# Fused attention and MLP on one Trainium2 core: global outputs kept in the score banks, AV of batches 0 and 1 unit by unit, the last output tile in two column halves

## The chip, the core and the metric

The kernel runs on one core of a Trainium2 chip. The metric is the time of one execution on the device, in microseconds (us); lower is better. Six runs of the kernel before gave 316.4 to 318.26 us, median 316.57 us.

The engines are named as in the profile: PE (TensorE matmul), PEld (its weight loads), DVE (VectorE), ACT (ScalarE), POOL (GpSimd) and SP (SyncE). A queue with a q at the end (SPq, ACTq, POOLq) is the part of an engine that issues its DMAs.

## The reference, cut to what matters

There are 8 batches, 8 heads, 512 local and 32 global tokens of 64 elements. Local queries see the 32 global keys and the local keys within 32 positions; global queries see everything. The result goes through a two-layer MLP.

```
s_g   = scale * q_g @ concat(k_g, k_l)^T            # 32 global queries x 544 keys
out_g = softmax(s_g) @ concat(v_g, v_l)
s_ll  = scale * q_l @ k_l^T, masked to |i - j| <= 32
s_lg  = scale * q_l @ k_g^T
out_l = softmax(concat(s_lg, s_ll)) @ concat(v_g, v_l)
x     = concat(out_g, out_l)                        # [8 * 544, 512]
h     = x @ w_in                                    # [4352, 2048]
out   = (h * sigmoid(1.702 * h)) @ w_out            # [4352, 512], float32
```

## The kernel before, in words

The program is written in the order in which each engine executes it: nothing reorders it, so an engine that waits holds back everything behind it in its own queue. Waits between engines come from the tiles that instructions read and write.

**Attention.** A `Quad` is four heads of one batch; quad `a` of a batch holds heads 0 to 3 and quad `c` heads 4 to 7. Its steps are methods:

- `T` (`Tk`, `Tq`) transposes keys and queries on DVE, and `ext` copies the global queries beside the local ones (four small DVE copies, one for each key window).
- `S(0)` and `S(1)` are the two rounds of score matmuls (16 each, row group by row group) into one 4-bank PSUM tile from the pool `psS`, which has a single buffer; `S(0)` ends with 8 small matmuls `gk` (global queries by global keys).
- `X` takes exp of a round on ACT (one large instruction, and in round 0 a small one for the `gk` columns), `M` multiplies the mask on DVE, `eg` builds a block-diagonal copy of the global part.
- `K` (8 matmuls) gives the scores of local queries by global keys in a bank `kb`, and `XK` its exp `ek`.
- `ekU(unit)` and `U(unit)` accumulate AV in a bank `ov` for each of three units: unit 0 is the row sum (ones as weights), units 1 and 2 the even and odd half of the values. `ekUs` does the three `ekU` in a row.
- `Gm` (16 + 4 matmuls) gives the global outputs in a bank `og`.
- `R` on DVE turns the row sum around, inverts it and spreads it (`sT`, `rT`, `rs`); `XL(0)` and `XL(1)` scale units 1 and 2 into the MLP input `xL`; `G` scales the global outputs into `xG` (three DVE instructions `rg`, `xg`, `xG`). `UG` is `ekUs`, the three `U` and `Gm`; `RXG` is `R`, `XL(0)`, `XL(1)`, `G`.

The banks `kb`, `ov`, `og`, and those of the MLP (`hp`, `op`), share a PSUM pool `psP` of 4 banks, handed out in turn.

**MLP.** `h_step(i, fc)` computes one of 16 blocks of the hidden layer of batch i: 4 matmuls of 128x512 into `hp`, tanh on ACT (`th`, two buffers), and one DVE instruction to `gT`. `o_mm` accumulates four of the 16 matmuls of one of the four output tiles of a batch in `op`; after the last of them `o_out` copies `op` to `ob` on ACT and SP issues four DMAs. Batch index 8 stands for the 256 global tokens of all batches.

**Order.** Batch 0's attention runs first, while the weights come in over POOL's DMA queue; PE runs dummy matmuls (`keep`) until the first scores are ready. Batch 1's attention is woven into the output tiles of batch 0 (`osteps`). From batch 2 on, `phase_o(i)` weaves the attention of batch i + 1 into the output tiles of batch i: `o(0)`, `c.S(0)`, `a.UG(c)`, `o(1)`, `c.S(1)`, `o(2)`, `a2.S(0)`, `c.UG(a2)`, `o(3)`, where `a2` is the first quad of batch i + 2; the hidden layer of batch i + 1 follows without interruption. In its last call there is no `a2`. The hidden layer of batch 1 contains `a.S(0)`, `a.K`, `a.X(0)`, `a.XK` of batch 2 after block 3, `M(0)` after 5 and `eg` after 7; `a.T` and `a.ext` of batch 2 stand ahead of block 0. At the end the hidden blocks of the global tokens alternate with the output tiles of batch 7, and the two output tiles of the global tokens come last.

Of the kernel before, what the change touches and what calls it, by code (L numbers as in the profile page):

```python
# [20 lines left out]
def kernel(  # L21
# [138 lines left out]
    def keep(n, ps):  # L160
        for _ in range(n):
            nc.tensor.matmul(ps, lhsT=warm[:, 0:128], rhs=warm, start=True, stop=True)

    keep(17, psP.tile([128, 512], F32, name="w", tag="p"))
# [43 lines left out]
    def transpose_g(lo, hi):  # L208
        for dst, s in ((kgT, rkg), (qgT, rqg)):
            nc.vector.transpose(dst[:, lo:hi, :32], s[:, lo:hi].bitcast(F32))  # L210
# [24 lines left out]
    class Quad:  # L235
        def __init__(self, Q):
# [11 lines left out]
            self.st = {}  # L248

# [16 lines left out]
        def ext(self):  # L266
            for (r0, nr), t0, n in zip(WIN, (0, 20, 1, 20), (4, 3, 3, 4)):
# [4 lines left out]
        def S(self, rnd, split=False, warm=0):  # L272
# [3 lines left out]
            else:  # L276
                pt = psS.tile([128, 4, 512], F32, name="s4")
# [15 lines left out]
            if rnd == 0:  # L293
                self.gk(ps[2][:, RW : RW + 32], self.qg)
# [14 lines left out]
        def X(self, rnd):  # L309
            e = self.E[rnd]  # L310
            if isinstance(self.ps, list):
                for j in range(4):
                    nc.scalar.activation(e[:, j, :RW], self.ps[j][:, :RW], AF.Exp, scale=scale)  # L313
                return
            nc.scalar.activation(e[:, :, :RW], self.ps[:, :, :RW], AF.Exp, scale=scale)  # L315
            if rnd == 0:
# [13 lines left out]
        def eg(self):  # L330
# [3 lines left out]
                self.E[0][:, 2, RW:].rearrange("p (o w) -> p o w", o=1).to_broadcast([128, 4, 32]))  # L334
# [15 lines left out]
        def ekUs(self, nxt=None):  # L350
            if nxt:
                nxt.K(0)
# [21 lines left out]
        def Gm(self):  # L374
            og = pbank("og")
# [36 lines left out]
        def UG(self, nxt=None):  # L412
            self.ekUs(nxt)
            for unit in range(3):
                self.U(unit)
            self.Gm()
# [46 lines left out]
    def o_out(i, tci, op):  # L463
        ob = moe.tile([128, d_model], F32, name="ob", bufs=6)
        nc.scalar.activation(ob, op, AF.Copy, scale=0.5)  # L465
        if i < B:
            rows = out[i * S + Sg : (i + 1) * S, :].rearrange("(r t) m -> t r m", t=16)
            for j in range(4):
                nc.sync.dma_start(out=rows[4 * tci + j], in_=ob[32 * j : 32 * j + 32, :])
        else:  # L470
            for j in range(4):
                r = (4 * tci + j) * S
                nc.sync.dma_start(out=out[r : r + Sg, :], in_=ob[32 * j : 32 * j + 32, :])
# [18 lines left out]
    cast_g32(0, "qk")  # L492
    transpose_g(0, 2)
    a.ext()
    a.Tq(0, 8)
    a.Tq(8, 16)
    a.Tk((0, 1))
    a.Tk((2, 3))
    load_rest()
# [10 lines left out]
    c.Tq()  # L510
    c.S(0)
# [4 lines left out]
    a.ekUs(c)  # L516
# [12 lines left out]
    c.eg()  # L529
    gTs[0] = moe.tile([128, FC, TB], BF16, name="gT")  # L530
    pt = pts[0] = psS.tile([128, 4, 512], F32, name="s4")
    c.ekUs()
    for unit in range(3):
        c.U(unit)
    c.R()
    for fc in range(4):
# [40 lines left out]
    a.S(0)  # L577
    a.K()
# [4 lines left out]
    osteps(0, (0, 2), (0, 3))  # L583
# [143 lines left out]
```

The softmax here doesn't subtract the row's maximum and nothing guards it: scores larger than these inputs give would overflow.

## Time and profile before

| | |
|---|---|
| median of six runs | 316.57 us (316.4 to 318.26) |
| the profiled execution's own time | 316.4 us |
| its span, first to last instruction | 314.7 us |
| PE busy / DVE busy / ACT busy / POOL busy | 298.3 / 211.0 / 165.8 / 79.9 us |
| instructions on PE / DVE / ACT | 3154 / 462 / 253 |
| mean granted PE clock | 0.995 of full speed |

Outside the span lie 1.7 us of the profiled execution's own time. A matmul's end in the profile is modelled: 128x512 matmuls are shown 379 ns long, but follow each other every 0.216 us, so a PE that is shown busy can still have lost time between two starts. A row of the timeline gives start, time until the last end, engine, line, operation, output <- inputs, shape, how many were merged (x), and in brackets the idle time before it and who ended it. A few per cent of the matmul records are missing, so a count of 15 can stand for 16.

### The profile page before, as it was taken

How to read it: one execution, taken by the hardware profiler on the slowest of the kernel's cores; microseconds unless marked ns; L12 is line 12 of the kernel's file. 1: busy time of each engine (PE TensorE's matmuls, PEld its weight loads, DVE VectorE, ACT ScalarE, POOL GpSimd, SP SyncE). 2: the span in 40 equal slices, each digit the busy share in tenths (PEclk: the TensorE clock that was granted, in tenths of full speed). 3: DMA queues.
4: the chain of work that ended last, by engine and by line, in shares of the span. 5: the costliest groups of instructions: out<-in, count | busy, mean ns of one | idle time of the engine just before them, and what ended most of it. 6: DMA issues, size and time to landing. Idle time of an engine off the chain costs nothing.

```text
span 314.7 us, 7687 instructions
## 1 busy us (share of the span) xinstructions
PE 298.3 (95%) x3154; PEld 144.4 (46%) x3189; DVE 211.0 (67%) x462; ACT 165.8 (53%) x253; POOL 79.9 (25%) x131
## 2 busy tenths in 40 slices
PE   6779999999999999999999999999999998999993
PEld 2344444444554455444454455445454454446651
DVE  7787946977866866776857866776677755673310
ACT  4717483386536745466446645566356650663420
POOL 8912588676146000900054002100000000000000
PEclk9999999999999999999999999999999999999998
DMA  8999999999969211970289113901120022101122
GB/s 154 156 196 205 207 158 180 166 133 108 164 77 164 47 35 44 155 106 18 53 79 172 20 35 69 102 0 35 36 60 10 0 52 52 33 2 33 35 67 68
DMA packets 59907, 27.44 MB, mean 87 GB/s; under 512 B 43232, under 2 KB 51424, under 8 KB 59872
## 3 DMA queue, kind: packets, MB, share of 16 engines
q0 software_dynamic: 51536, 17.11, 50.2%
q1 hardware_dynamic: 7904, 9.25, 12.0%
q10 hardware_dynamic: 432, 0.59, 0.6%
q8 instruction: 25, 0.41, 0.6%
q14 instruction: 10, 0.08, 0.1%
HBM read 35.13 MB, written 8.91 MB: 140 GB/s over the span
## 4 chain that ended last, share of the span: by engine, by line
PE 73%; DMA 10%; POOL 8%; DVE 4%; issue 2%; ACT 1%; POOLq 0%; ACTq 0%
PE op L458 34%; PE hp L433 30%; DMA w_out_sb<-in_moe_w_out_dram 9%; PE s L286 4%; POOL rk L84 3%; DVE sT L391 3%; POOL v L97 2%; PE ov L347 2%; PE ov L368 2%; DMA v<-in_v_l_dram 2%; POOL w_in_sb L217 1%; DVE gT L441 1%; ACT th L440 1%; PE kb L305 0%; PE s L305 0%
## 5 line engine op out<-in xcount | busy, mean ns | idle before, releaser
L458 PE MATMUL op<-w_out_sb,gT 128*128 128x512 bf16 x519 | 123.2, 379 | 2.9 <-DVE xL L400 0.8
L441 DVE SCALAR_TENSOR_TENSOR gT<-th,hp 128x512 bf16<-128x512 f32 (+1 forms) x140 | 91.0, 656 | 42.4 <-ACT th L440 41.7
L433 PE MATMUL hp<-xL,w_in_sb 128*128 128x512 bf16 x487 | 108.2, 379 | 0.6
L440 ACT ACTIVATE th<-hp 128x512 f32<-128x512 f32 (+1 forms) x140 | 79.9, 573 | 43.1 <-PE hp L433 39.3
L433 PEld LDWEIGHTS <-w_in_sb 128*128 128x128 bf16 x576 | 56.1, 98 | 65.1 <-issue 1.3
L458 PEld LDWEIGHTS <-gT 128*128 128x128 bf16 x544 | 51.6, 98 | 59.1 <-issue 4.1
L465 ACT ACTIVATE ob<-op 128x512 f32<-128x512 f32 x34 | 20.3, 597 | 77.6 <-PE op L458 77.5
L315 ACT ACTIVATE e<-s 128x1712 bf16<-128x1712 f32 x31 | 49.4, 1595 | 6.0 <-PE s L305 5.5
L97 POOL DMA_DIRECT2D v<-in_v_l_dram x36 | 26.9, 753 | 95.0 <-PE og L385 88.8
L84 POOL DMA_DIRECT2D rk<-in_k_l_dram x64 | 34.9, 557 | 15.5 <-DMA w_in_sb<-in_moe_w_in_dram 5.9
L391 DVE STREAM_TRANSPOSE sT<-ov 128x512 f32<-128x512 f32 x16 | 11.5, 717 | 34.4 <-PE ov L368 34.4
L322 DVE TENSOR_TENSOR e<-e,mask 128x1408 bf16<-128x1408 bf16 x32 | 27.9, 872 | 7.1 <-ACT e L315 6.9
L286 PE MATMUL s<-q,kT 32*128 32x200 bf16 (+1 forms) x512 | 21.3, 284 | 2.7 <-DVE kT L256 1.4
L400 DVE TENSOR_TENSOR xL<-ov,rs 128x512 bf16<-128x512 f32 x32 | 20.7, 684 | 1.5
L286 PEld LDWEIGHTS <-kT 32*128 32x128 bf16 x512 | 11.0, 95 | 16.8 <-issue 10.1
L338 ACT ACTIVATE ek<-kb 128x512 bf16<-128x512 f32 x16 | 9.6, 603 | 7.0 <-PE kb L305 7.0
L368 PE MATMUL ov<-e,v 128*32 128x192 bf16 (+1 forms) x512 | 12.5, 239 | 0.0
L347 PE MATMUL ov<-ek,rvg 32*32 32x512 bf16 x128 | 10.0, 375 | 1.9 <-DVE xL L400 1.9
L395 DVE STREAM_TRANSPOSE rs<-rT 128x512 f32<-128x512 f32 x16 | 11.4, 711 | 0.6
L256 DVE STREAM_TRANSPOSE kT<-rk 128x512 f32<-128x512 f32 (+1 forms) x17 | 11.3, 669 | 0.1
L259 DVE STREAM_TRANSPOSE q<-rq 128x512 f32<-128x512 f32 (+1 forms) x17 | 10.9, 644 | 0.3 <-DMA rq<-in_q_l_dram 0.3
L305 PE MATMUL kb<-q,kgT 32*32 32x512 bf16 x128 | 10.0, 385 | 0.6 <-ACT e L313 0.6
(64 smaller groups left out, 142.5 us busy)
## 6 DMA issues: line engine op xcount, KB each, us to landing
out_dram<-ob SPq DMA_DIRECT2D x136, 64.0 KB, 1.8
rk<-in_k_l_dram POOLq DMA_DIRECT2D x64, 64.0 KB, 4.2
v<-in_v_l_dram POOLq DMA_DIRECT2D x28, 128.0 KB, 4.4
rq<-in_q_l_dram POOLq DMA_DIRECT2D x6, 512.0 KB, 6.8
w_in_sb<-in_moe_w_in_dram POOLq DMA_DIRECT2D x4, 512.0 KB, 11.8
w_out_sb<-in_moe_w_out_dram POOLq DMA_DIRECT2D x4, 512.0 KB, 13.4
rq<-in_q_l_dram POOLq DMA_DIRECT2D x3, 256.0 KB, 8.0
q<-in_q_l_dram ACTq DMA_DIRECT2D x1, 512.0 KB, 4.1
```

The source lines that it names most:

```text
L84: nc.gpsimd.dma_start(out=loaded[b][0][32 * j : 32 * j + 32, u], in_=kf[b, j][:, u])
L97: nc.gpsimd.dma_start(out=vtiles[b % 2][p, s, :, :, :D], in_=vf[b, t][:, hs])
L286: nc.tensor.matmul(ps[j][:, off : off + n * nr], lhsT=self.k[p, 128 * c : 128 * c + 128, e], rhs=self.q[p, t0 : t0 + n, r0 : r0 + nr, e], ...
L315: nc.scalar.activation(e[:, :, :RW], self.ps[:, :, :RW], AF.Exp, scale=scale)
L322: nc.vector.tensor_mul(e, e, mask[:, rnd : rnd + 1, :].to_broadcast([128, 4, LW]))
L391: nc.vector.transpose(sT.rearrange("p a b -> p (a b)"), self.st[0])
L400: nc.vector.tensor_mul(self.x[:, 2 * self.u + h, :], self.st[1 + h], self.st["rs"])
L433: nc.tensor.matmul(hp[:, : width(i)], lhsT=w_in_c[:, fc // 8, kc, fc % 8 // 2, :, fc % 2], rhs=(xL[i] if i < B else xG)[:, kc, :], start=( ...
L440: nc.scalar.activation(th[:, :n], hp[:, :n], AF.Tanh, scale=0.851)
L441: nc.vector.scalar_tensor_tensor(gTs[i][:, fc, :n], in0=th[:, :n], scalar=1.0, in1=hp[:, :n], op0=ALU.add, op1=ALU.mult)
L458: nc.tensor.matmul(op, lhsT=gTs[i][:, fc, tci * 128 : tci * 128 + 128], rhs=w_out_sb[:, fc, :], start=(first and fc == 4 * f4), stop=(fc = ...
L465: nc.scalar.activation(ob, op, AF.Copy, scale=0.5)
```

## The change

- The dummies ahead of the first scores: 62 of 128 columns in the place of 17 of 512.
- The start of batch 0: cast and transpose of the global keys move behind the transposes of queries and local keys, and two of the four `ext` copies behind the first half of the key transpose. In the split round `S(1)` of quad 0 `gk` now comes with that round, and its exp takes the extra columns of bank 2; the small separate exp goes.
- `gk` is a step of its own (`gg`) at the head of `ekUs(nxt)`, or after `a.S(0)`; it writes to the same place of the score tile as before.
- `Gm(nxt)` writes the global outputs to 66 free columns of bank 0 of the next quad's score tile, in the place of a bank of `psP`; `RXG` of a quad now stands behind `XK` and `X(0)` of the next one in the program.
- AV of the second quad of batch 0 and of batch 1, and of the last quad, goes unit by unit (`ekU(0)`, `U(0)`, `ekU(1)`, `U(1)`, ...).
- Batch 1's steps and batch 0's output tiles are woven in another order. In the hidden layer of batch 1, `a.T` of batch 2 moves from ahead of block 0 to behind block 3, the transposes of the globals and `ext` behind block 5, `S(0)`, `gg`, `K`, `XK`, `X(0)` behind block 7, `M(0)` and `eg` behind block 10.
- The last output tile is computed in two halves of 256 columns, each with its own bank, copy and four DMAs; in the second half two of the DMAs are issued by ACT.

```diff
-    keep(17, psP.tile([128, 512], F32, name="w", tag="p"))
+    keep(62, psP.tile([128, 512], F32, name="w", tag="p"), 128)
...
+        def spt(self, rnd):
+            if rnd or self.pt is None:
+                pt = psS.tile([128, 4, 512], F32, name="s4")
+                if rnd:
+                    return pt
+                self.pt = pt
+            return self.pt
+
+        def gg(self):
+            self.gr = 0
+            self.gk(self.spt(0)[:, 2, RW : RW + 32], self.qg)
...
         def ekUs(self, nxt=None):
             if nxt:
+                nxt.gg()
                 nxt.K(0)
...
-        def Gm(self):
-            og = pbank("og")
+        def Gm(self, nxt=None):
+            og = nxt.pt[:, 0, RW : RW + D + 2] if nxt else pbank("og")
...
         def UG(self, nxt=None):
-            self.ekUs(nxt)
+            if nxt:
+                self.ekUs(nxt)
             for unit in range(3):
+                if not nxt:
+                    self.ekU(unit)
                 self.U(unit)
-            self.Gm()
+            self.Gm(nxt)
...
+        last = i == B and tci == B // 4 - 1
+        for lo, hi in ((0, 256), (256, 512)) if last else ((0, 512),):
+            if last:
+                op = pbank("op")
+                for fc in range(FC):
+                    nc.tensor.matmul(op[:, lo:hi], lhsT=gTs[i][:, fc, tci * 128 : tci * 128 + 128],
+                                     rhs=w_out_sb[:, fc, lo:hi], start=(fc == 0), stop=(fc == FC - 1))
+            nc.scalar.activation(ob[:, lo:hi], op[:, lo:hi], AF.Copy, scale=0.5)
             for j in range(4):
+                eng = nc.scalar if lo and j % 2 else nc.sync
...
-    cast_g32(0, "qk")
-    transpose_g(0, 2)
-    a.ext()
+    cast_g32(0, "q")
+    transpose_g(0, 2, "q")
+    a.ext((0, 1))
     a.Tq(0, 8)
     a.Tq(8, 16)
     a.Tk((0, 1))
+    a.ext((2, 3))
     a.Tk((2, 3))
+    cast_g32(0, "k")
+    transpose_g(0, 2, "k")
...
-    c.ekUs()
     for unit in range(3):
+        c.ekU(unit)
         c.U(unit)
     c.R()
+    c.eg()
...
     a.S(0)
+    a.gg()
     a.K()
...
-    osteps(0, (0, 2), (0, 3))
+    osteps(0, (2, 1), (2, 0), (0, 2), (0, 3))
     a.S(1)
     a.X(1)
     c.T()
     a.M(1)
     osteps(0, (1, 2), (1, 3))
+    osteps(0, (2, 2))
     c.S(0)
-    c.X(0)
-    c.M(0)
-    c.eg()
-    osteps(0, (2, 0), (2, 1), (2, 2), (2, 3))
-    c.S(1)
-    c.X(1)
+    osteps(0, (2, 3))
     a.ekUs(c)
     c.XK()
-    for unit in range(3):
-        a.U(unit)
+    c.X(0)
+    a.U(0)
+    a.R()
+    osteps(0, (3, 0))
+    a.U(1)
+    a.U(2)
+    c.S(1)
     a.Gm()
-    a.R()
-    c.M(1)
     a.XL(0)
     a.XL(1)
     a.G()
-    osteps(0, (3, 0), (3, 1))
+    c.M(0)
+    c.eg()
+    c.X(1)
+    c.M(1)
+    osteps(0, (3, 1), (3, 2))
     c.UG()
     c.RXG()
-    osteps(0, (3, 2), (3, 3))
+    osteps(0, (3, 3))
     a, c = nq[2]
-    a.T()
-    transpose_g(4, 6)
-    a.ext()
...
     for fc in range(FC):
         h_step(1, fc)
         if fc == 3:
+            a.T()
+        if fc == 5:
+            transpose_g(4, 6)
+            a.ext()
+        if fc == 7:
             a.S(0)
+            a.gg()
             a.K()
+            a.XK()
             a.X(0)
-            a.XK()
-        if fc == 5:
+        if fc == 10:
             a.M(0)
-        if fc == 7:
             a.eg()
...
         c.S(0)
         a.UG(c)
-        a.RXG()
         c.XK()
         c.X(0)
+        a.RXG()
...
             c.UG(a2)
+            a2.XK()
+            a2.X(0)
         else:
...
-            c.ekUs()
             for unit in range(3):
+                c.ekU(unit)
                 c.U(unit)
...
-    for st in range(FC // 2):
+    for st in range(4):
         o_mm(B, st)
+    o_out(B, 1, None)
```

## The prediction

> **What bounds the kernel now.** The page first: PE is busy in every slice from the third on, at the full clock, so a change counts only where PE starts a matmul later than it could.
>
> ```profile
> PE   6779999999999999999999999999999998999993
> PEclk9999999999999999999999999999999999999998
> ```
>
> The waits of PE name the stalls: banks of `psP` that DVE has not read yet (L347, L458), and the first scores (L286).
>
> ```profile
> PE ov L347 <- DVE xL L400: 1.9, 3, 1.0
> PE s L286 <- DVE kT L256: 1.4, 1, 1.4
> PE op L458 <- DVE xL L400: 0.8, 1, 0.8
> ```
>
> Then the timeline, at the places that the change touches. The start: first scores, second half of w_in, and the matmuls that need it.
>
> ```profile
> 8.28 0.67 PE L286 MATMUL s<-q,kT 32*128 32x200 bf16 x16 [1.43 <-DVE kT L256]
> 21.89 0.10 PEld L433 LDWEIGHTS <-w_in_sb 128*128 128x128 bf16 x1 [0.18 <-DMA w_in_sb<-in_moe_w_in_dram]
> 22.40 1.89 PE L433 MATMUL s<-xL,w_in_sb 128*128 128x512 bf16 x8 [0.20 <-DVE xL L400]
> ```
>
> The hidden layer of batch 1 (ACT's tanh, DVE's gT, then the scores of batch 2):
>
> ```profile
> 58.19 3.62 PE L433 MATMUL hp<-xL,w_in_sb 128*128 128x512 bf16 x16
> 59.25 0.60 ACT L440 ACTIVATE th<-hp 128x512 f32<-128x512 f32 x1 [0.27 <-PE hp L433]
> 61.13 2.69 DVE L441 SCALAR_TENSOR_TENSOR gT<-th,hp 128x512 bf16<-128x512 f32 x4
> 61.74 0.66 PE L286 MATMUL s<-q,kT 32*128 32x200 bf16 x16
> ```
>
> A later batch, from unit 0 of `a` to `c.S(1)`:
>
> ```profile
> 113.87 0.49 PE L368 MATMUL ov<-e,ones 128*32 128x160 bf16 x16
> 114.41 0.72 DVE L391 STREAM_TRANSPOSE sT<-ov 128x512 f32<-128x512 f32 x1 [2.31 <-PE ov L368]
> 114.93 0.20 PE L385 MATMUL og<-rvg,eg 128*32 128x66 bf16 x4
> 115.18 3.61 PE L458 MATMUL op<-w_out_sb,gT 128*128 128x512 bf16 x15
> 117.66 0.28 DVE L407 TENSOR_SCALAR xg<-og,rg 128x64 bf16<-128x64 f32 x1
> 118.72 0.67 PE L286 MATMUL s<-q,kT 32*128 32x228 bf16 x16
> ```
>
> The last quad, and the end:
>
> ```profile
> 264.43 0.38 PE L458 MATMUL op<-w_out_sb,gT 128*128 128x512 bf16 x1 [0.80 <-DVE xL L400]
> 306.77 5.28 SPq L473 DMA_DIRECT2D out_dram<-ob  x8
> 309.60 0.60 ACT L465 ACTIVATE ob<-op 128x512 f32<-128x512 f32 x1 [2.86 <-PE op L458]
> ```
>
> **Later batches: 11 x 0.12 = 1.32 us gained.** Four `og` matmuls are followed by the next work after 0.125 us when nothing is waited for (24.36 to 24.50), but by `op` after 0.25 (114.93 to 115.18): `op` gets the bank of unit 0 and waits for `sT`, which ends at 115.13. With `og` out of `psP`, the built order gives `op` the bank of `kb`, freed by XK (113.81 + 0.60 = 114.41): no wait. This happens twice in each of five `phase_o` and once in the sixth. What is late next: in the score bank `Gm` stands before X(0) in the program, and X(0) (one access over all four banks) waits for it, so X(0) moves from 114.30 to 115.2, its small exp ends at 117.0; `rg` waits for that, but starts at 117.47 anyway; `c.S(1)` now waits for `xg`, done at 117.95, and wants to start at 118.72 - 0.12 = 118.60. Slack 0.65, cost nothing. The Trainium skill ("PSUM — Partial Sum Buffer", PSUM bank collisions raise a hardware error) speaks against this placement: two engines may not touch one bank in the same partitions at once, whatever the columns, so `Gm` and X(0) must take turns. In the rows `og` at 114.80 to 115.13 lies inside X(0) (114.30 to 115.89), in different banks; by the rule the turn costs ACT 0.9 us, which is the move already counted, and PE nothing.
>
> **Start: 0.43 us gained, not more.** Ahead of the first scores DVE loses one cast, one transpose and two copies. From the cast of the queries (done 6.24): transpose 6.28, two copies 6.53 and 6.63, two query transposes 6.73 and 7.09, first half of the keys 7.42 to 7.82; first scores 7.87 for 8.28. The landed keys (four DMAs, the last at 7.03) allow it. `gk` no longer stands before X(0): 8.60 for 9.15; quad 1's scores 11.80 for 12.35, its X(0) 12.52 for 13.22, its `S(1)` 14.25 for 14.96, its `ekU(0)` 15.74 for 16.45. There unit by unit acts: `U(0)` waits for the mask of round 1 (`M(1)` on DVE, done 17.75), unit 1 follows at 17.97, unit 2 needs the bank of `XL(1)` (18.36), and PE is through at 19.3 for 20.5. The 8 hidden matmuls on the first half of w_in end at 21.03; the second half of w_in lands at 21.85 whatever PE does (the row at 21.89 waits for it). They go on at 21.97 for 22.40, since `xL` is then ready at 20.8. So 0.86 us of the lead is lost to the DMA, and it also covers the dummies. These run 0.427 us each until 4.62 us, when the clock is granted, then 0.216. No row has 128 columns with full weights; bounds are a quarter of 512 columns (0.107 and 0.055) and the length of a weight load (0.147 and 0.098): the train would end at 6.4 or at 8.7. I take 6.4, since weight loads lie beside matmuls in all rows; at 8.7 the first scores come 0.8 later, still under the cover. The skill's "TensorE: Matmul & The Clock Gate" (Back-to-back issue gap) has two figures for 128 columns, 56 ns isolated and 81 ns sustained; by them the train would end at 6.4 or 7.3, both before 7.87; no run here shows it.
>
> **Batch 1: 0.43 shrinks to 0.14.** Scores at 38.26 for 38.68. Four groups of four `op` matmuls (0.863 each, 0.10 for a change of shape) put `S(1)` at 43.02; `w_out` for the third and fourth group has landed (37.7, 40.2) long before. Three more groups, `c.S(0)` at 46.31, `op(2, 3)` to 47.87. Three `op` tiles now hold banks: `ekU(2)` waits for the copy of the third (its last matmul ends 47.94, copy to 48.58), costing 0.27; `U(0)` at 48.94, `sT` at 49.48. From `sT` to the end of `xG` DVE takes 3.75 (the spacings 55.41 to 59.16), and only then come `c.M(0)` (53.23 to 54.10) and, after `eg`, `c.M(1)` (54.13 to 55.02). PE has `op(3, 0)`, units 1 and 2, `c.S(1)`, `Gm` and two groups, done at 53.6, then `ekU(0)`; `c.U(0)` waits for both masks until 55.08, about 1.0 lost. Its `sT` starts at 55.46. Unit by unit costs two more changes of shape, some 0.2; `op(3, 3)` ends at 57.6, but the hidden layer's first bank is that of unit 1, read by `XL(0)` until 58.00. It starts at 58.05 for 58.19. The old stalls of this stretch (about 2 us, at `og`, `ekU`, `op`) are thus replaced.
>
> **Hidden layer of batch 1: from 0.14 ahead to 0.87 behind.** This is where the change costs. A `gT` starts 1.70 after its step does (59.89 for the step at 58.19: 0.86 + 0.20 + 0.60 + 0.04). Steps take 0.863, so gT3 starts at 62.35, `a.T` behind it runs 62.95 to 64.18, gT4 and gT5 follow at 0.60 each, the transposes at 65.38, the first `ext` copy ends at 65.87. `a.S(0)` stands on PE behind block 7, which is through at 65.05: it waits 0.87. Before, the copies were done at 61.2 when PE arrived at 61.64. After it X(0) (1.59) and XK (0.60) stand before tanh 8, and the two `th` buffers tie tanh n to gT n - 2; with `M(0)` (0.77) behind gT10 the bank of block 15 comes free 0.3 late and that of block 12 0.1 late. The stall of 0.27 that this layer had goes. Together 1.0 lost; `S(1)` at 74.56 for 73.69.
>
> **Last quad: 0.45.** Before, three `ekU` take 0.757 before `U(0)`; now one takes 0.305. The chain sT, rT, rs, `XL(0)` (2.55) that frees the bank of the next `op` starts 0.45 earlier, and PE arrives before it ends, so all of it shows.
>
> **End: 0.8.** Matmuls of 256 columns follow each other every 0.109, so two halves cost what the whole did; the last ends 0.04 later. The copy takes 0.38 for 0.60 (tanh of 256 columns as the row). Four issues at 0.36 to 0.47 put the last one 1.30 after the first, landing 1.81 later at 313.33; now SP still has the first half's DMAs to issue until about 310.3, then two; the last starts near 310.75 and lands at about 312.5.
>
> **Sum.** 0.87 - 1.32 - 0.45 - 0.80 = -1.70, from 316.40 to 314.70 in the profiled execution; its time is 0.17 under the median of 316.57, so 314.9 as a median. A measurement here tells 0.3%, 0.95 us, from no change: faster is below 315.62, slower above 317.52.
>
> **Rivals.** (1) `a.S(0)` in the hidden layer does not wait: DVE gets to the copies in time. For it: gT's mean is 656 ns and some start early; against it: the 1.70 of every step. Worth 0.87: 314.0. Chance 0.18. (2) DVE's backlog there grows: from gT4 on 12 steps at the unhidden 0.69 in place of 0.60 add up to 1.1, and every tanh behind X(0) hands it on; 316.0, no change. Chance 0.20. (3) Slower: `c.S(1)` waits for `xg` in the shared score bank in six batches. It decides from 0.65 us of delay in the chain sT to xg; at 1.1 it costs 0.45 x 6 = 2.7 and the time is 317.6. Against it: DVE is idle before `sT` (2.31 in the row). Chance 0.05. The forecast keeps 0.57. That the change does not do what it says is excluded by the built order, which shows `op` waiting for XK.
>
> Range: down to rival 1 with 0.7 more if the start and batch 1 stall less than worked out, 313.3; up through rival 2 to 316.3.
>
> **What would show it.** Right: no 0.12 gap after `og`; the start held by w_in at 21.9; a wait of PE s on DVE q near 65 of about 0.9; SP's last issue near 310.7 less the gain. Wrong: a wait of `s` for `xg` in every batch, a clock granted later than 4.6, or `S(1)` of batch 2 earlier than 73.7.

## The result, and the profile after

The changed kernel takes 315.06 us (median of 24 runs, 313.95 to 316.32), where the kernel before, run beside it, takes 317.44 us (median of 50 runs, 316.21 to 320.97). The ratio is 0.9929, with a 95% interval of 0.9915 to 0.9943: 0.6 to 0.9% faster. The profiled execution of the changed kernel takes 314.89 us, 1.51 us less than that of the kernel before (316.40); their spans are 313.2 and 314.7 us. The forecast was 314.9 us, in a range of 313.3 to 316.3.

The page shows what it showed before: PE busy almost everywhere and the clock granted.

```profile
PE   8679999889999999999999999999999999999994
PEclk9999999999999999999999999999999999999999
```

The waits of PE (total us, times, longest us) are what has changed. The banks of `psP` that DVE had not read (1.9, 0.8 and parts of others before) are gone. In their place stand two transfers, the masks, and the `ext` copies.

```profile
PE ov L387 <- DVE e L328: 1.1, 2, 0.6
PE s L455 <- DMA w_in_sb<-in_moe_w_in_dram: 0.8, 1, 0.8
PE ov L387 <- DMA v<-in_v_l_dram: 0.8, 1, 0.8
PE s L291 <- DVE q L273: 0.7, 1, 0.7
```

The timeline of the changed kernel at the places that the prediction showed; first the start. The first scores come 0.37 earlier. But U(1) of quad 0 now waits for v, and the hidden matmuls on the second half of w_in wait for that half and start at 22.40, as before.

```profile
7.90 0.67 PE L291 MATMUL s<-q,kT 32*128 32x200 bf16 x16
15.85 0.80 PE L387 MATMUL ov<-e,v 128*32 128x160 bf16 x32 [0.80 <-DMA v<-in_v_l_dram]
19.92 1.67 PE L455 MATMUL s<-xL,w_in_sb 128*128 128x512 bf16 x7 [0.16 <-issue]
22.40 1.90 PE L455 MATMUL s<-xL,w_in_sb 128*128 128x512 bf16 x8 [0.81 <-DMA w_in_sb<-in_moe_w_in_dram]
```

The hidden layer of batch 1: eight blocks in one row, then the scores of batch 2, which wait for the copies of `ext`, a second wait (0.19) for the bank of the last block, and `S(1)` at 74.86 for 73.69.

```profile
58.42 7.07 PE L455 MATMUL hp<-xL,w_in_sb 128*128 128x512 bf16 x32
66.19 0.67 PE L291 MATMUL s<-q,kT 32*128 32x200 bf16 x16 [0.71 <-DVE q L273]
73.91 1.02 PE L455 MATMUL hp<-xL,w_in_sb 128*128 128x512 bf16 x4 [0.19 <-DVE gT L463]
74.86 0.67 PE L291 MATMUL s<-q,kT 32*128 32x228 bf16 x16
```

A later batch: `op` starts 0.13 behind the start of the four last matmuls of the global outputs (now `s<-rvg,eg`, since they lie in the score bank), in place of 0.25. `X(0)` waits for them (0.80), as worked out, and `xg`, done at 118.90, is 0.7 ahead of `c.S(1)`.

```profile
115.89 0.20 PE L404 MATMUL s<-rvg,eg 128*32 128x66 bf16 x4
116.02 3.63 PE L480 MATMUL op<-w_out_sb,gT 128*128 128x512 bf16 x15
116.17 1.60 ACT L321 ACTIVATE e<-s 128x1712 bf16<-128x1712 f32 x1 [0.80 <-PE s L404]
118.62 0.28 DVE L426 TENSOR_SCALAR xg<-s,rg 128x64 bf16<-128x64 f32 x1
119.58 0.67 PE L291 MATMUL s<-q,kT 32*128 32x228 bf16 x16
```

The last quad (no wait in front of `op`), and the end: a copy of 0.38, and ACT issues two of the DMAs of the second half.

```profile
264.02 3.63 PE L480 MATMUL op<-w_out_sb,gT 128*128 128x512 bf16 x16
302.92 7.97 SPq L502 DMA_DIRECT2D out_dram<-ob  x14
309.25 0.38 ACT L494 ACTIVATE ob<-op 128x256 f32<-128x256 f32 x1 [1.36 <-PE op L492]
309.66 0.82 ACTq L502 DMA_DIRECT2D out_dram<-ob  x2
```

Stage by stage, from the starts of PE's rows (the last landing from the transfers):

| mark | before | after | lead so far | lead forecast |
|---|---|---|---|---|
| first scores | 8.28 | 7.90 | 0.37 | 0.41 |
| hidden matmuls, second half of w_in | 22.40 | 22.40 | 0.00 | 0.43 |
| first scores of batch 1 | 38.68 | 38.60 | 0.08 | 0.42 |
| first hidden matmul of batch 1 | 58.19 | 58.42 | -0.23 | 0.14 |
| `S(1)` of batch 2 | 73.69 | 74.86 | -1.17 | -0.87 |
| `c.S(1)` of batch 7 | 257.24 | 257.25 | -0.01 | 0.45 |
| first hidden matmul of batch 7 | 267.88 | 267.49 | 0.39 | 0.90 |
| last landing | 313.33 | 312.05 | 1.28 | 1.70 |

### The profile page after: what moved, and what is told of

Same layout as the page of the kernel before. It is cut to its first block, busy times and chain, and to the rows that moved or that the text cites. A ratio compares the mean times of both kernels' runs of the same rounds, so it can differ in the third digit from the quotient of the medians.

```text
span 313.2 us, 7832 instructions
## 1 busy us (share of the span) xinstructions
PE 299.5 (96%) x3214; PEld 148.9 (48%) x3250; DVE 210.8 (67%) x462; ACT 167.2 (53%) x253; POOL 79.9 (26%) x131
## 4 chain that ended last, share of the span: by engine, by line
PE 84%; DVE 5%; DMA 4%; POOL 3%; issue 2%; ACT 2%; DVEq 0%; POOLq 0%; ACTq 0%
PE op L480 35%; PE hp L455 33%; PE s L291 5%; PE ov L387 5%; DMA w_in_sb<-in_moe_w_in_dram 4%; PE ov L365 2%; POOL rk L84 1%; DVE gT L463 1%; PE op L492 1%; POOL v L97 1%; ACT th L462 1%; PE kb L310 1%; DVE e L328 1%; PE s L455 1%; PE s L310 1%
## 5 line engine op out<-in xcount | busy, mean ns | idle before, releaser
L480 PE MATMUL op<-w_out_sb,gT 128*128 128x512 bf16 x503 | 119.8, 380 | 1.8 <-issue 0.8
L480 PEld LDWEIGHTS <-gT 128*128 128x128 bf16 x528 | 49.1, 98 | 56.2 <-issue 3.5
L494 ACT ACTIVATE ob<-op 128x512 f32<-128x512 f32 (+1 forms) x35 | 20.5, 585 | 64.5 <-PE op L480 62.0
L387 PEld LDWEIGHTS <-v 128*32 128x32 bf16 x512 | 9.9, 97 | 2.9 <-issue 2.9
```

The costliest lines, as they stand in the source:

```text
L387: nc.tensor.matmul(ov[32 * j : 32 * j + 32, :].rearrange("p (t r) -> p t r", t=16)[:, :, r0 : r0 + nr], lhsT=lv, rhs=self.E[c // 2][:, j, ...
L480: nc.tensor.matmul(op, lhsT=gTs[i][:, fc, tci * 128 : tci * 128 + 128], rhs=w_out_sb[:, fc, :], start=(first and fc == 4 * f4), stop=(fc = ...
L494: nc.scalar.activation(ob[:, lo:hi], op[:, lo:hi], AF.Copy, scale=0.5)
```

## The experiments

Unless said otherwise each kernel is the changed one with the edit that is shown. In their traces the stretches from batch 1 on that an edit does not touch repeat within 0.02 us from kernel to kernel, so a stretch between two marks can be compared directly. There is one exception: in the first of the two last versions batch 1 takes 19.97 for 19.81, because PE waits 0.16 for the last quarter of w_out, which lands at 41.87. The ratios are to the kernel before, in runs on the same chip.

### The weave in the hidden layer of batch 1, alone undone

```diff
+    a.T(); transpose_g(4, 6); a.ext()      # ahead of block 0
     for fc in range(FC):
         h_step(1, fc)
...
-        if fc == 7:
+        if fc == 3:
             a.S(0); a.gg(); a.K()
...
```

> The changed kernel with one part undone: in the hidden layer of batch 1 the steps of batch 2 stand again where they stood before (transposes and ext ahead of block 0, scores, K and exps behind block 3, mask behind 5, eg behind 7). My theory: this weave is the part that costs. In the changed kernel the stretch from the first hidden matmul of batch 1 to S(1) of batch 2 takes 16.45 us, before it took 15.51; undone, it should take 15.5 again, the wait of PE s on DVE q (0.7 in the waits of PE, behind the last ext copy) should be gone, and the time be 0.94 us below the changed kernel's: about 0.989 to 0.990 of the kernel before, where the changed one has 0.993. Rival: the weave was moved because batch 1's second quad now ends later on DVE (its R, XL, G); then the transposes and ext, put back ahead of block 0, hold up gT 0 to 3, PE waits for banks there, and the stretch stays at 16.2 to 16.5, time unchanged.

Measured: ratio 0.9922 (0.9902 to 0.9943), median 314.37 us, profiled execution 314.03 us. The start happens to be the same (block 4 at 24.52 and 24.51), and so is the first hidden matmul of batch 1 (58.42 in both). From there to `S(1)` of batch 2 pass 15.57 us for 16.45:

```profile
58.42 3.61 PE L455 MATMUL hp<-xL,w_in_sb 128*128 128x512 bf16 x16
61.97 0.66 PE L291 MATMUL s<-q,kT 32*128 32x200 bf16 x16
63.17 10.88 PE L455 MATMUL hp<-xL,w_in_sb 128*128 128x512 bf16 x48
73.99 0.67 PE L291 MATMUL s<-q,kT 32*128 32x228 bf16 x16
```

The row at 61.97 has no idle time ahead of it: the wait for `ext` is gone. The weave costs 0.88 us in the trace, and the rival, that DVE's later end of batch 1 takes it back, falls. The ratio's interval alone would not have told it from the changed kernel.

### Global outputs in the pool again

```diff
-            self.Gm(nxt)
+            self.Gm()
```

> The changed kernel with one part undone: the global outputs of all quads go to a bank of the pool psP again; every other order stays. My theory: from batch 2 on, 'op' behind the 'og' matmuls gets the bank of unit 0 again and waits for sT, 0.12 us each time (0.25 in place of 0.125 from the last og to op), 11 times: 1.2 to 1.3 us slower than the changed kernel, about 0.997 of the kernel before. Rival: the score bank gives something else too or instead (X(0) of the next quad is held by Gm and reorders ACT); then the spacing behind og does not change and the time moves by less than 0.5.

Measured: ratio 0.9980 (0.9956 to 1.0005), median 316.16 us. `op` waits again and starts 0.25 behind the start of the four last `og` matmuls, at eleven places from batch 2 on:

```profile
116.19 0.20 PE L404 MATMUL og<-rvg,eg 128*32 128x66 bf16 x4
116.44 3.61 PE L480 MATMUL op<-w_out_sb,gT 128*128 128x512 bf16 x16
```

From `S(1)` of batch 2 to `c.S(1)` of batch 7 the kernel before takes 183.55 us, this one 183.54, the changed one 182.39. So the whole lead of the later batches, 1.15 us or 11 times 0.105, belongs to this one edit.

### The last output tile in one piece

```diff
-        for lo, hi in ((0, 256), (256, 512)) if last else ((0, 512),):
...
+        nc.scalar.activation(ob, op, AF.Copy, scale=0.5)
...
-    for st in range(4):
-        o_mm(B, st)
-    o_out(B, 1, None)
+    for st in range(FC // 2):
+        o_mm(B, st)
```

> The changed kernel with one part undone: the last output tile is computed, copied and stored in one piece again. My theory: the last matmul ends 0.04 earlier, the copy takes 0.60 in place of 0.38, and four issues on SP of 0.36 to 0.47 follow it, so the last landing comes 3.75 to 3.85 us after the last matmul's start, where the halves have it at about 2.95: 0.85 to 0.9 us slower than the changed kernel, 0.9955 to 0.996 of the kernel before. Rival: the end is set by the transfers alone (1.6 to 1.8 us from issue to landing) and the halves only gain the copy's 0.22: 0.2 to 0.3 slower.

Measured: ratio 0.9972 (0.9954 to 0.9989). From the first hidden matmul of the globals to the last landing pass 31.64 us, in the changed kernel 30.75: the halves are worth 0.90. The copy alone saves 0.22. Another 0.48 is the chain of issues: the last one starts 1.33 behind the end of the last copy here, where all four are on SP, and 0.85 behind it in the changed kernel. The last transfer saves 0.24: it carries half as much in the changed kernel and lands 1.57 behind its issue, for 1.81 here. The last copy starts 0.04 later there, which takes a little back.

```profile
303.16 8.73 SPq L494 DMA_DIRECT2D out_dram<-ob  x12
309.44 0.60 ACT L487 ACTIVATE ob<-op 128x512 f32<-128x512 f32 x1 [2.86 <-PE op L480]
```

### The halves alone, in the kernel before

The same edit the other way round, in the kernel before.

> The kernel before with one part of the change alone: the last output tile in two column halves. My theory: 0.85 to 0.9 us faster than the kernel before (0.997), all of it behind the last hidden matmul of the globals; the stretch from the first hidden matmul of the globals to the last landing falls from 31.64 to 30.75. It also shows the start of the kernel before a second time: if v lands at 11.8, 12.8, 13.8, 14.8 and the second half of w_in at 21.85 again, the later landings of the changed kernel (12.2, 14.0, 15.2, 15.7; 22.36) come from the change; if it shows the late ones too, they change from execution to execution, and the first hidden matmuls of batch 0 still follow the same path, since they wait for xL at 22.4 there. I expect the second. Rival for the end: less than 0.3 gained, since the transfers set the end.

Measured: ratio 0.9991 (0.9962 to 1.0021), which decides nothing; the trace does: 30.74 us for 31.64 from the first hidden matmul of the globals to the last landing, 0.90 again. The start of the kernel before is seen a second time here: v lands at 12.75, 13.75, 14.73 and 15.63 (11.81 to 14.75 in its first profile), the second half of w_in at 22.09 (21.85), and the hidden matmuls on it start at 22.54, still held by `xL`. So late landings come in the kernel before too, and cost it little.

### The start as before

```diff
-    keep(62, psP.tile([128, 512], F32, name="w", tag="p"), 128)
+    keep(17, psP.tile([128, 512], F32, name="w", tag="p"))
...
-    cast_g32(0, "q"); transpose_g(0, 2, "q"); a.ext((0, 1))
+    cast_g32(0, "qk"); transpose_g(0, 2, "k"); transpose_g(0, 2, "q"); a.ext()
...
```

> The changed kernel with one part undone: 17 dummies of 512 columns, and key and query globals cast and transposed together with all four ext copies ahead of the query transposes, as before. First scores about 0.4 later (8.28 for 7.90). My theory: in the profiled run PE then still waits for the second half of w_in, or is just in time for it, so the matmuls on it start where they did (22.4), and the time is that of the changed kernel within 0.1 us (0.993 of the kernel before). Rival: in most executions the second half of w_in lands earlier than in the profiled one (22.36; in the profile of the kernel before 21.85), so the lead is worth up to 0.43 there, and the time is 0.3 to 0.45 us above the changed kernel's (0.9945). A third way: the 62 short dummies delay the grant of the clock or add instruction fetches that delay the early transfers (three quarters of v landed 1.0 to 1.4 later in the changed kernel's profile); then the time is below the changed kernel's and v lands at 12.8, 13.8 and 14.8 again.

Measured: ratio 0.9940 (0.9916 to 0.9964). The first scores are back at 8.29, yet block 4 starts at 23.88, earlier than in the changed kernel (24.51). In this execution the second half of w_in lands at 21.60, and PE goes through both halves without a wait:

```profile
20.05 3.63 PE L455 MATMUL s<-xL,w_in_sb 128*128 128x512 bf16 x16
```

So in this pair of profiles the landing of w_in decides when block 4 starts, and not the lead of 0.39. What lowers it from 24.50 in the kernel before to 23.88 with the same start is, by the rows of DVE, another part: AV of the second quad unit by unit. `XL` starts at 20.59 in this run and at 21.66 in the kernel before (the second fence), since `U(0)` no longer stands behind all three `ekU`. From `S(0)` of quad 1 to block 4 pass 11.48 us here, 12.15 and 12.07 in the two profiles of the kernel before. That is read from the rows; no run isolates it.

```profile
20.59 1.29 DVE L419 TENSOR_TENSOR xL<-ov,rs 128x512 bf16<-128x512 f32 x2
```

```profile
21.66 1.29 DVE L400 TENSOR_TENSOR xL<-ov,rs 128x512 bf16<-128x512 f32 x2
```

Whether the lead is worth something where w_in lands early, as the rival has it, this pair cannot tell: w_in landed 0.76 later in the profile with the lead, and the interval holds 0.9929 and the rival's 0.9945 alike. The third way is not shown: v lands late with the long dummies too (12.73 to 15.17 here, 12.75 to 15.63 in the run above). It is not excluded either, since the last v landed at 15.45 to 16.18 in the six profiles that have the short dummies and this order of transfers, and at 14.75 to 15.63 in the three that have the long ones.

### Batch 1 and the weave as before

```diff
-    osteps(0, (2, 1), (2, 0), (0, 2), (0, 3))
+    osteps(0, (0, 2), (0, 3))
     a.S(1)
...
```

> The changed kernel with two parts undone: the order of batch 1 and the weave in the hidden layer of batch 1. The first run of this kind, with the weave alone undone, shortened the stretch from the first hidden matmul of batch 1 to S(1) of batch 2 from 16.45 to 15.57 us. My theory: the new order of batch 1 costs too; from the first scores of batch 1 to the first hidden matmul the changed kernel takes 19.81 us, the kernel before took 19.51, because c.U(0) waits for both masks on DVE (0.8) and shape changes are added, which eats what the old order lost at banks. Undone: 19.5 again, hence 0.3 below the run with the weave alone undone, 1.2 below the changed kernel, about 0.989 of the kernel before. Rival: the gain of the new order is hidden by something later (op behind og still waits for sT there); then undone it is 19.8 or more, and the time that of the run with the weave alone undone.

Measured: ratio 0.9899 (0.9871 to 0.9928), median 313.97 us. From the first scores of batch 1 to the first hidden matmul pass 19.82 us, not 19.5: my theory fell. The old order computes (0, 2) and (0, 3) as soon as batch 1's scores are out, and waits for the last quarter of w_out there. That quarter lands at 40.96 here, at 41.09 in the kernel before with the halves, and at 40.21 in its first profile, before PE needs it. The row of the kernel before with the halves shows the wait:

```profile
41.13 1.02 PE L458 MATMUL op<-w_out_sb,gT 128*128 128x512 bf16 x4 [0.15 <-DMA w_out_sb<-in_moe_w_out_dram]
```

From the first of the eight `op` matmuls behind `K` to `S(1)` pass 2.14 here, 2.15 in the kernel before with the halves, and 1.83 in its first profile. So the new order takes as long as the old one when w_out is late, and 0.3 longer when it is early.

### Transfers in another order

```diff
-        load_v(0)
+        load_v(0, (0,)); load_v(0, (1,))
...
+        for q in range(2):                 # columns q * 512 to q * 512 + 511
+            for u in range(2):
+                nc.gpsimd.dma_start(out=w_in_sb[:, 0, 2 * u : 2 * u + 2, cs], in_=w_in_r[u][:, :, cs])
```

> The changed kernel with another order of the first transfers: v of batch 0 by quads (the four DMAs of quad 0 first), and the first half of w_in by columns, so that the first 512 columns, which the first four hidden blocks need, come for all of K before the next 512. My theory: in the changed kernel the start is set by transfers, not by the dummies, transposes and score order: in its profile U(1) of quad 0 waits for v (0.8) and the hidden matmuls for the second half of w_in (0.8), and every execution lands them at other times. With the new order both waits go or fall under 0.3, and hp of block 4 starts at 23.3 to 23.8 in place of 24.51: 0.7 to 1.2 us faster than the changed kernel, 0.990 of the kernel before. Rival: DVE is next (U(0) of the second quad waits for the mask M(1), then XL), so PE is held until 22 all the same and hp starts at 24.2 or later; or the smaller DMAs (64 KB and 256 KB) land later in sum and the wait moves to block 4 and on.

Measured: ratio 0.9996 (0.9973 to 1.0020): a miss. The first hidden matmul starts at 21.86:

```profile
21.86 2.33 PE L459 MATMUL s<-xL,w_in_sb 128*128 128x512 bf16 x10 [0.89 <-DMA w_in_sb<-in_moe_w_in_dram]
```

The second w_in DMA had landed at 19.84; 21.82 is the third, whose columns these matmuls do not read. In the next kernel it is 22.33 and 22.37. I read this as waits put on stretches: the first 512 columns of two K blocks lie with the other columns between them. A later kernel gives each block of columns a stretch of its own. The granted clock is at half from 13.54 to 16.95 us in this execution, but the wait of 0.89 comes behind that, so the landing decides all the same. The profiled execution (316.02 us) is one of the five shorter ones of twelve; the other seven took 317.36 to 318.33 us, and no profile shows why.

### A first version to beat both

It has that load order, the old weave, `c.Gm` of batch 0 ahead of the second half of w_in, and a new order of batch 1:

```diff
     c.S(0)
-    osteps(0, (2, 3))
-    a.ekUs(c)
-    c.XK()
+    c.gg()
     c.X(0)
+    c.M(0)
+    osteps(0, (2, 3))
...
```

> A version to beat both: the changed kernel with the weave of the hidden layer of batch 1 as before, the new order of loads, c.Gm of batch 0 ahead of the hidden matmuls on the second half of K, and another order of batch 1: the global scores of its second quad straight behind S(0), X(0) ahead of XK, M(0) ahead of R of the first quad, M(1) ahead of G, and its last global outputs in the score bank of batch 2's first quad. My theory: from the first scores of batch 1 to the first hidden matmul 18.8 to 19.2 us (19.81 in the changed kernel), since DVE was idle until sT of the first quad and M(0) then lies there, so that c.U(0) no longer waits for M(1) (0.8); 15.5 in the hidden layer; 0.7 to 1.2 at the start. Together 2.3 to 2.8 below the changed kernel: 312.2 to 312.8, 0.985 to 0.987 of the kernel before. Rival: M(0) ahead of R delays sT, R and the banks behind it, and what c.U(0) gains is lost at the banks of the output tiles; then the stretch stays at 19.5 to 19.8 and the sum at 313.

Measured: ratio 0.9983 (0.9957 to 1.0009), no gain over the changed kernel. The loads cost 1.5 us (block 4 at 26.01), batch 1 takes 19.70, since `ekU(2)` waits 0.75 for the copy of the output tile, which now stands behind `X(0)` on ACT, and the hidden layer takes 16.01, since DVE reaches its first `gT` late. The rival had named the second (19.5 to 19.8).

### w_in in four tiles

```diff
-    w_in_sb = wts.tile([128, 2, NKC, d_ff // 2], BF16)
+    w_in_sb = wts.tile([128, 4, NKC, d_ff // 4], BF16)
...
+        for q in range(4):
+            for u in range(2):
+                nc.gpsimd.dma_start(out=w_in_sb[:, q, 2 * u : 2 * u + 2, :], in_=w_in_r[u][:, :, q * 512 : (q + 1) * 512])
```

> The changed kernel with w_in held as four tiles of 512 columns and loaded by them, so that the first four hidden blocks need only the first two of the DMAs (256 KB each) in place of 1 MB. The earlier try at this kept the old tile, where the first block of columns of a pair of K blocks is not one stretch; there the first hidden matmul started 45 ns after the third w_in DMA landed (21.82 and 21.86; 22.33 and 22.37), a DMA whose data it does not read, so it did not test the theory. My theory: from its start PE needs the two DMAs by 20 and 21.7, they land by 19 and 20.5, and hp of block 4 starts at 23.7 to 24.0, in every execution, where the changed kernel has 23.88 to 24.74 by the landing of w_in: 0.3 to 0.8 us below the changed kernel, 0.990 to 0.992 of the kernel before. Rival: XL(1) of the second quad on DVE is just as late as w_in; then hp starts at 24.3 or later and the time does not move.

Measured: ratio 0.9922 (0.9896 to 0.9949), median 314.10 us, 7 of the 11 runs between 313.78 and 314.19. The profiled execution is its slowest (316.85 us) and cannot show the start: the granted clock is at half in it from 17 to 24 us, and the stretch from the first hidden matmul to block 4 takes 4.80 (3.61 in the next kernel). Columns: window, its length, busy us and instructions of PE, PEld, DVE, ACT and POOL, granted clock, DMA share, GB/s.

```profile
16.00:18.00 2.00, 1.75 (x64) 1.22 (x65) 1.74 (x3) 0.86 (x1) 1.25 (x2) 0.80 1.13 159
18.00:20.00 2.00, 1.80 (x32) 0.67 (x28) 1.93 (x5) 0.00 (x0) 1.27 (x2) 0.50 1.20 186
```

What it was to show is in the next two kernels, which load w_in in the same way, and v by quads besides. The narrow times fit the theory, but the interval holds the changed kernel's 0.9929 too.

### Two versions to beat both

The first: the old weave, w_in in four tiles, v by quads, `eg` of the second quad of batch 0 behind its `XL`.

> A version to beat both: the changed kernel with the weave of the hidden layer of batch 1 as before, w_in in four tiles as in the run with w_in by columns, v of batch 0 by quads, and eg of the second quad of batch 0 behind its XL. My theory: the gains add: 0.88 in the hidden layer of batch 1, 0.6 to 0.9 at the start (hp of block 4 at 23.6 to 23.9, without the wait of U(1) for v): 1.5 to 1.8 below the changed kernel, 0.987 to 0.988 of the kernel before. Rival: the 12 more DMAs in front of batch 1's loads make its keys late and PE waits in batch 1 for S(0) or w_out what it gained; then the time is that of the run with the weave alone undone (0.992).

Measured: ratio 0.9884 (0.9847 to 0.9920), median 313.35 us. PE waits neither for v nor for w_in; block 4 starts at 23.77:

```profile
20.16 3.40 PE L461 MATMUL s<-xL,w_in_sb 128*128 128x512 bf16 x15 [0.16 <-issue]
```

The second has a new order of batch 1 as well, with `S(0)`, `X(0)` and `M(0)` of the second quad one output step earlier than in the first attempt:

```diff
     osteps(0, (1, 2), (1, 3))
-    osteps(0, (2, 2))
     c.S(0)
-    osteps(0, (2, 3))
+    c.gg(); c.X(0); c.M(0)
+    osteps(0, (2, 2), (2, 3))
...
+    nq[2][0].spt(0)
+    c.Gm(nq[2][0])
+    nq[2][0].Tk()
     c.RXG()
```

> As the version before this one, and with another order of batch 1: S(0), global scores, X(0) and M(0) of its second quad stand ahead of the output step (2, 2), where ACT and DVE have nothing to do (DVE is idle for 3.2 us ahead of sT in the changed kernel), its last global outputs go to the score bank of batch 2's first quad, and the key transpose of that quad stands ahead of R. In an earlier try S(0) stood one output step later and ekU(2) waited 0.7 for the copy of the output tile behind X(0) on ACT. My theory: c.U(0) waits for M(1) 0.3 at most (0.8 in the changed kernel), op behind og waits no more, and from the first scores of batch 1 to the first hidden matmul 18.7 to 19.1 us pass (19.81); the hidden layer takes 15.2 to 15.6: 0.7 to 1.1 below the version before this one, 0.984 to 0.985 of the kernel before. Rival: the wait at ekU(2) or at the banks of the output tiles stays, 19.5 or more, and the two versions are equal.

Measured: ratio 0.9876 (0.9834 to 0.9917), median 312.79 us; profiled execution 312.32 us, the shortest of this study. From the first scores of batch 1 to the first hidden matmul pass 19.07 us for 19.81, the hidden layer takes 15.56. `M(0)` lies where DVE was idle, and the matmuls of `c.U(0)` follow each other with at most 0.17 between two starts, where the changed kernel has one of 0.85. The intervals of the two versions overlap; only the traces tell them apart. Both beat the kernel before by at least 0.8%; that they beat the changed kernel is likely from the medians, but the intervals touch its own (0.9915 to 0.9943).

### The start as before, without the waits for transfers

The first of these two versions with the start undone, by the same edit as above.

> The first of the two versions to beat both (weave of the hidden layer of batch 1 as before, w_in in four tiles, v of batch 0 by quads) with the lead undone: 17 dummies of 512 columns, and the key globals and all ext copies ahead of the query transposes, as in the kernel before. The question is whether the earlier first scores (7.90 for 8.28) are worth anything now that PE no longer waits for v and w_in. My theory: no; the next thing that binds is the queries of quad 1, which land at 11.2 to 11.8 and are transposed then, so that its S(0) starts at 12 to 12.5 in both, and hp of block 4 starts within 0.15 us of 23.77; time as that version (0.988). Rival: with the transfers out of the way all of the 0.39 is handed on by DVE (sT of quad 0 to XL of quad 1 run without a break), hp starts at 24.1 to 24.2 and the time is 0.4 higher (0.9895).

Measured: ratio 0.9905 (0.9879 to 0.9932), median 313.79 us. First scores at 8.29 for 7.90, `S(0)` of quad 1 at 12.20 for 12.29, block 4 at 23.76 for 23.77. Between these two profiles the lead is worth nothing, though no transfer of v or w_in is waited for: it is gone by the query transpose of quad 1, at 11.44 here and at 11.52 there. There the row waits for the transfer of these queries, which landed at 11.50 (at 10.47 here).

```profile
11.52 0.71 DVE L269 STREAM_TRANSPOSE q<-rq 128x512 f32<-128x512 f32 x1 [0.39 <-DMA rq<-in_q_l_dram]
```

The second version has the same start as the first, and in its profile the queries landed at 11.26:

```profile
11.29 0.71 DVE L269 STREAM_TRANSPOSE q<-rq 128x512 f32<-128x512 f32 x1
12.05 0.66 PE L297 MATMUL s<-q,kT 32*128 32x200 bf16 x16 [0.64 <-DVE q L269]
```

Its block 4 starts at 23.53, 0.23 earlier than without the lead. From `S(0)` of quad 1 to block 4 pass 11.48 us in both versions and 11.56 here. So the lead is worth what the transfer of these queries leaves of it, nothing in one profile and 0.23 in the other; they land between 10.47 and 12.04 in the 14 profiles. The medians (313.79, and 313.35 with the lead) and the ratio lie where the rival has them, 0.4 above the version with the lead, but the intervals overlap. Theory and rival each hold for some landings, and what the lead is worth on average stays open.

## Why the prediction was right, and which terms were not

**Hidden layer of batch 1.** Forecast: 16.51 us from its first matmul to `S(1)` of batch 2 (58.05 to 74.56), with `a.S(0)` held by the last `ext` copy. Measured 16.45, with that wait at that place, 0.71 long for 0.87, and a second one of 0.19 at the bank of block 15, which the forecast had at 0.3; undone, 0.88 came back. Rival 1 (no wait) and rival 2 (a backlog growing behind `gT` 4) are out.

**Batch 1.** Forecast: 19.79 from its first scores to the first hidden matmul; measured 19.81. Its 1.0 at `c.U(0)` was 0.85. What the step took wrongly is the other side: the 19.51 of the kernel before was an early landing of w_out; two later runs of the old order took 19.82 and 19.83.

**Later batches.** Forecast 1.32, measured 1.15: the bank and the count of 11 were right. The rows show the wait of 0.12 at each place (0.25 for 0.13), but the stretch gains only 0.105 for each; the rest was not traced. The slower rival, `c.S(1)` waiting for `xg`, kept a distance of 0.7.

**Start: the step that failed.** It took 0.43, on the ground that w_in lands at 21.85 "whatever PE does". In this profile it landed at 22.36, and PE gained nothing. The landing was treated as a constant and is a variable: in the six kernels that keep the changed kernel's order of transfers block 4 started at 23.88 once and at 24.51 to 24.74 five times, held in four of these by w_in. In the fifth (batch 1 and the weave as before) w_in landed in time, at 21.68; there `U(1)` started at 16.12, behind the last v, which landed at 15.98, and the granted clock was at half from 16.21 to 19.62 us, so that PE took 4.78 us from `U(1)` to the first hidden matmul for 4.07 in the changed kernel.

The step was also silent on the transfer of quad 1's queries, which landed at 11.15 here (its scores came at 11.94, forecast 11.80). Even in kernels that wait for no v or w_in, the lead of the first scores reaches block 4 only as far as that transfer leaves it: nothing of it when the queries landed at 11.50, and 0.23 at 11.26. The unit order lowers block 4 by 0.62, by the rows, and the landings of v and w_in decide how much of that is had.

The clock's grant, taken as 4.62, came at 7.12. The prediction had named a later grant as a sign of being wrong; it cost nothing, because the last dummy started at 7.57, between the bounds of 6.4 and 8.7. In a kernel whose dummies ended at 6.36 (the first version to beat both) the first scores started at 7.92 all the same.

**Last quad and end.** 0.45 forecast, 0.40 measured (from a lead of -0.01 to 0.39; no run undoes this part alone). The end 0.80 forecast, 0.89 measured and 0.90 twice by experiment: the sum let the last transfer land 1.81 behind its issue, and it landed 1.57 behind it.

**The sum.** 1.70 forecast, 1.51 measured in the profiled pair. Too much by 0.43 at the start, 0.16 in the later batches, and 0.08 in batch 1 and the last quad; too little by 0.23 behind the last landing (the span ends 1.14 behind it, before 1.36), 0.09 each at the end and ahead of the first scores of batch 1, and 0.07 in the hidden layer. That 315.06 lies so close to 314.9 is in part luck: these errors nearly cancel, the 0.23 was not in the forecast at all, and the kernel before, put at 316.57, has a median of 317.44 here.

The medians are 2.38 apart, more than the profiles. The kernel before was profiled near its floor (316.40, lowest 316.21, median 317.44), the changed one at its median (314.89 and 315.06). The granted clock that is listed with each run goes with the long runs of the kernel before. In 83 of its runs beside the experiments, the 25 with a mean clock of at most 0.993 took 316.97 us or more, median 317.56; the 39 with at least 0.998 took at most 317.37, median 316.63. Of the changed kernel's 24 runs one alone has so low a clock (0.987), the slowest at 316.32. So a part of the 2.38 goes with a clock that fell back in the kernel before; no profile shows such a run of it, and whether the change prevents it stays open. The landings of w_in and v move block 4 by 0.85 in the six profiles, while the 24 runs of the changed kernel spread over 2.4 us; they explain a part of that at most.

**The turn at the score bank.** The turns of `Gm` and `X(0)` at the score bank (the Trainium skill, "PSUM — Partial Sum Buffer", PSUM bank collisions raise a hardware error) show in the row of `X(0)` at 116.17, held by PE for 0.80. ACT pays; PE does not, since `c.S(1)` at 119.58 has no wait ahead of it.

## What to carry to other kernels

Ask of each landing that a step rests on how far it may move, and take the time that PE needs it as one end and the latest landing in any profile as the other: a lead ahead of a transfer is worth only what the transfer leaves. A matrix multiplication that stalls behind a bank can be freed by another home for a small output, if the turn that this home enforces falls on an engine with slack. And a step moved from ahead of a run of matmuls into it must be priced by its place in the queue of the engine that does it: here 1.9 us of transposes and copies, set between the `gT` of the hidden layer, cost PE 0.88.

## What the runs showed of the hardware

- The time at which PE's dummies go to full speed changes from execution to execution: the last half-speed start lies between 3.58 and 7.10 us in 14 profiles, while PE starts at 1.47 in all that recorded the first one. The short dummies follow each other every 0.107 us and then every 0.056.
- In three of the 14 profiled executions the clock went back to half early in the kernel: from 17.21 to 24.04 us (w_in in four tiles), from 16.21 to 19.62 (batch 1 and the weave as before) and from 13.54 to 16.95 (transfers in another order), though the longest step between two starts on PE just before was 1.31, 1.25 and 1.30 us. The Trainium skill ("TensorE: Matmul & The Clock Gate", HAM oscillation — how this bites in real kernels) asks for no idle gap of more than about 3.4 us; by that rule alone the clock would have stayed up here, so it is not the whole condition.
- What the traces show instead is PE's busy share in a window. The stretches of full and half clock that end within these 14 profiles are whole multiples of 3.41 us. In the 3.41 us ahead of each of the three drops PE is shown busy for 1.78, 1.85 and 1.82 us (rows in pairs, ahead of the drop and behind it, in the order above; the second number is PE's busy time, the third from the end the granted clock):

```profile
13.80:17.21 3.41, 1.78 (x81) 1.38 (x72) 2.88 (x5) 2.79 (x4) 2.18 (x4) 1.00 1.22 152
17.21:20.62 3.41, 3.21 (x48) 1.14 (x52) 3.34 (x7) 0.00 (x0) 1.44 (x3) 0.50 1.18 182
12.79:16.21 3.42, 1.85 (x60) 0.94 (x47) 2.49 (x9) 3.14 (x4) 2.37 (x4) 1.00 1.51 160
16.21:19.62 3.41, 3.41 (x84) 2.17 (x87) 2.94 (x5) 0.58 (x1) 1.08 (x3) 0.50 1.09 192
10.13:13.54 3.41, 1.82 (x60) 1.13 (x60) 2.55 (x7) 2.62 (x7) 3.03 (x5) 1.00 2.03 139
13.54:16.95 3.41, 3.41 (x84) 1.95 (x69) 1.71 (x4) 2.90 (x4) 2.72 (x4) 0.50 1.24 135
```

  Cut into such windows from the grant on, some 1260 in all, the 14 profiles have no drop behind a window in which PE is busy for more than 1.85 us. Of the 11 windows between 1.66 and 1.85 us three are followed by one, and all 14 below 1.3 us, at the end of each kernel. So a window that is busy for about half goes with a drop without being enough for it. PE's busy time is modelled at its ends, and no run varies it on purpose.
- The last of four v transfers of batch 0, issued within 0.06 us of the same time, landed between 14.75 and 16.18 us in the nine profiles with that order of transfers; the queries of the second quad of batch 0, issued within 0.09 us, between 10.47 and 12.04 us in all 14.
